# Memory attention and a gated feed-forward block on one core: block products for the first two batches too

## The chip, the cores and the metric

One NeuronCore of a Trainium2 chip runs the whole kernel in one launch. TensorE multiplies matrices into eight PSUM banks, ScalarE and VectorE evaluate functions and move PSUM to SBUF, GpSimd works on SBUF alone and also issues the casting loads, SyncE issues most stores. The metric is the device time of one execution in microseconds; the median over 3 runs of the kernel before is 238.54 (238.09 to 239.02).

## The reference

Inputs: q, k, v of shape 8 x 8 x 576 x 64 (batch, head, token, head dimension), phi of 8 x 8 x 576 x 32, and weights of 512 x 1536 (gate, value) and 1536 x 512 (output).

```
a    = softmax(phi, over the 32 memory slots)
k_m  = a^T k ;  v_m = a^T v                  # 32 x 64 per batch and head
attn = softmax(q k_m^T / 8)                  # 576 x 32
x    = attn v_m, heads side by side          # 4608 x 512
out  = (silu(x w_gate) * (x w_val)) w_out    # 4608 x 512, float32
```

## The kernel before

**Stages.** Batches are handled one after the other, except that batches 0 and 1 are interleaved. For a batch the kernel (1) sums keys and values over tokens with the softmax weights of phi (`kv_items`, matmuls at L235, scaled by `kv_norm`, transposed by `kv_T`), (2) computes scores (L400) and their exponentials E, (3) instead of forming x multiplies the value memory into the weights, U = v_m W (`u_round`, L471), (4) normalises E to A (`z_inv_v` and `norm`: L434, L441, L443, L451, all VectorE), (5) forms gate and value as A U in 24 slots of 128 rows x 288 tokens (`gv_slots`, L514), ScalarE's silu (L531) and VectorE's product (L537) giving the hidden tile h, transposed, in three chunks of 512 rows, and (6) multiplies h by the output weights.

**Two forms of the output step.** In batches 0 and 1 (`FAST = 2`) the 512 first tokens of a batch are four units of 12 matmuls of 512 columns (`out_units`, L633), one bank and one copy to SBUF (L333, L331) each. In batches 2 to 7 `products` (L713) uses the Strassen-Winograd scheme on 2 x 2 blocks: seven products instead of eight, 12 matmuls of 256 columns each. They need block sums of h (`chunk_done`: four operations per chunk, chunks 0 and 1 on GpSimd, chunk 2 on VectorE; L598, L560) and of the output weights (`weight_sums`, VectorE, once for all batches, tiles t_T). Three banks, s, a and c, collect the products; p1, q6 and p5 are copies to SBUF by ScalarE (L736), c11, c12 and c22 additions by VectorE (L741), c21 a copy. A product that starts in a bank waits until the copy or addition before it has read that bank. The last 64 tokens of two batches are one `out_rest` (L661).

**Order.** Each engine runs its instructions in the order in which the program lists them, and waits are semaphores set by the framework from the tiles. The order is written by hand: a list `backlog` holds the output units, `take(n)` places the next n of them, and `spread` merges gate/value slots, backlog and the next batch's preparation by position. `run_late` runs what `late` holds. PSUM banks are handed out in rotation by `bank` and `done`.

**Loads.** GpSimd issues all casting loads in program order; each also waits until the load eight before it has landed. Queries live in two slots (`Q_SLOT`): batches 2 and 3 share slot 0, so batch 3's load waits until batch 2's queries have been transposed, by a DMA issued from SyncE (`load_qT`, L121). Batches 0 and 1 are transposed on TensorE instead (`q_T`, L377, copied out at L388 and L390). Tiles of h, phi and keys/values have two buffers each; tiles of U and of block sums have one per chunk, tags U and S.

**The end.** `store` writes 128 rows in pieces that follow the output's layout; after `box["end"]` is set, pieces alternate between SyncE's and ScalarE's queues.

The order of the middle part before the change, which the edit rewrites:

```
load_qT(2); phi_exp(2)
run(take(16)); weight_sums(0); run(take(12))
run(kv_items(2)[:1] + take(6) + kv_items(2)[1:] + take(7))
weight_sums(1); run(take(11))
```

Of the kernel before, what the change touches and what calls it, by code (L numbers as in the profile page):

```python
# [14 lines left out]
def kernel(  # L15
# [66 lines left out]
        for t in tiles:  # L82
            free.append(held.pop(id(t))[0])

    Q_SLOT = (0, 1, 0, 0, 1, 0, 1, 0)

    def head_pairs(x):

# [370 lines left out]
    def u_round(b, parts, evac):  # L459


        banks = []
        for which, c, halves in parts:
            w0, w1, h0, h1 = which[0], which[-1] + 1, halves[0], halves[-1] + 1
            n = (h1 - h0) * HC
            p = [bank([128, CH], FP32, f"p_u{g}") for g in range(NG)]
            for w in which:
                o = (w - w0) * n
                for i in range(NP):
                    for g in range(NG):  # L470
                        nc.tensor.matmul(  # L471
                            p[g][32 * i:32 * i + 32, o:o + n],
                            lhsT=kTs[b][64 * g:64 * g + 64, 2, 32 * i:32 * i + 32],
                            rhs=w_part(w, c, i, g, halves),
                            start=True,
                            stop=True,
                            tile_position=(64 * g, 32 * i),
                        )
            for g in range(NG):
                if (b, c, g) not in Us:  # L480
                    Us[b, c, g] = upool.tile([128, 2, 2, HC], BF16, tag=f"U{c}{g}", name="t_U")
                if len(which) == 1:
                    dst = Us[b, c, g][:, h0:h1, w0]
                else:
                    dst = Us[b, c, g][:, h0]
                src = p[g][:, 0:(w1 - w0) * n].rearrange("p (a f) -> p a f", f=HC)
                banks.append((dst, src, p[g], rSs[b][:, g:g + 1] if b in scaled else None))
        for (t, p, home, r), e in zip(banks, evac):
            if e == "a":
                if r is None:  # L490
                    nc.scalar.copy(out=t, in_=p)  # L491
                else:
                    nc.scalar.activation(out=t, in_=p, func=AF.Copy, scale=r)
            elif r is None:
                nc.vector.tensor_copy(out=t, in_=p)  # L495
            else:
                nc.vector.tensor_scalar(out=t, in0=p, scalar1=r, scalar2=None, op0=ALU.mult)
            done(home)
# [48 lines left out]
        gv_gate(b, s)  # L547
        flush_mul(n)

    def u_buffers(b):  # L550

        for c in range(NCH):
            t = upool.tile([128, NG, 2, 2, HC], BF16, tag=f"S{c}", name="t_U")
            for g in range(NG):
                Us[b, c, g] = t[:, g]

    xs, Ss, late = {}, {}, []

# [22 lines left out]
    def chunk_done(b, c):  # L581

        if b % 2 == 0 and c == 0:
            xs[b // 2] = hpool.tile([128, NJF, 2, 64], BF16, tag="xs", name="t_x")

        def ends():
            nc.gpsimd.tensor_copy(
                out=xs[b // 2][:, 4 * c:4 * c + 4, b % 2], in_=hts[b, c][:, :, S - 64:S]
            )

        if b < FAST:
            ends()
            return
        eng = nc.vector if c + 1 == NCH else nc.gpsimd
        t = upool.tile([128, 4, 2, 256], BF16, tag=f"S{c}", name="t_S")
        Ss[b, c] = t
        A11, A12, A21, A22 = blocks(b, c)
        eng.tensor_tensor(out=t[:, 0], in0=A21, in1=A22, op=ALU.add)  # L598
        subtract(eng, t[:, 1], t[:, 0], A11)
        subtract(eng, t[:, 2], A11, A21)  # L600
        subtract(eng, t[:, 3], A12, t[:, 1])
        if c + 1 < NCH:
            ends()
        else:
            late.append(ends)

    def token_segments(b, t0, count):
        segs = []
# [8 lines left out]
    def store(t_o, b, t0, count, row=0, cols=slice(0, 512), queues=None):  # L617
# [3 lines left out]
        for n, (r0, m, bb, jj, pp) in enumerate(token_segments(b, t0, count)):  # L621
            eng = queues[n % len(queues)] if queues else nc.sync
            eng.dma_start(out=out_r[bb, jj, pp:pp + m, cols], in_=t_o[row + r0:row + r0 + m])

    def out_units(b, u, eng):

        mine = {}

        def unit(jf):
            def run():  # L630
                if jf == 0:
                    mine["p"] = bank([128, DM], FP32, "p_oo")
                nc.tensor.matmul(  # L633
                    mine["p"],
                    lhsT=hts[b, jf // 4][:, jf % 4, 128 * u:128 * (u + 1)],
                    rhs=WO[jf],
                    start=(jf == 0),
                    stop=(jf == NJF - 1),
                )
                if jf == NJF - 1:  # L640
                    t_o = work.tile([128, DM], FP32, tag="to", name="t_o")
                    copy(eng, t_o, mine["p"])
                    done(mine["p"])
                    store(t_o, b, 128 * u, 128)

            return run

        return [unit(jf) for jf in range(NJF)]

    def out_rest(pair, half):  # L650

# [31 lines left out]
    def products(b, by_hand):  # L683
# [56 lines left out]
        def add(out, home, other, free=False):  # L740
            nc.vector.tensor_tensor(out=out, in0=mine[home], in1=mine[other], op=ALU.add)  # L741
            if free:
                done(mine[home])

        def c11():
            t = tile_of("o1", (128, 2, DM), tag="to")
            add(t[:, :, lo], "a", "p1", True)

        def c22():
            t = tile_of("o2", (128, 2, DM), tag="to")  # L750
            add(t[:, :, hi], "s", "p5")

        def c12():
            t = mine["o1"]
            add(t[:, :, hi], "c", "q6", True)
            for u in range(2):
                store(t[:, u], b, 128 * u, 128)

        def c21():
            t = mine["o2"]  # L760
            copy("v" if box.get("end") else "a", t[:, :, lo], mine["s"])
            done(mine["s"])
            for u in range(2):
                store(t[:, u], b, 256 + 128 * u, 128)

        ops = dict(
            p1=keep("p1", "s"), q6=keep("q6", "s"), p5=keep("p5", "c"),
# [9 lines left out]
        if b + 1 == B:  # L777
            return first + six + five + seven + three + four, ops
        return first + five + six + three + seven + four, ops

    FAST = 2

    def out_list(b):
        res = []
        for u in range(4):
            res += out_units(b, u, "a" if u < 2 else "v")
        return res

    def q_items(b, evac):
        return [  # L790
# [86 lines left out]
    load_phi(2, nc.gpsimd)  # L877
    load_wo(2)
    load_v(2)
    load_phi(3, nc.gpsimd)  # L880
    load_q(2)
    load_q(3)
    u_buffers(1)


    warm(104)
# [51 lines left out]
        run([u_item(1, c)] + g0[s + 5:s + 8] + g1[s:s + 5])  # L938
    run(g1[-3:])
    flush_mul()  # L940
    backlog = out_list(0) + out_list(1) + out_rest(0, 0)

    def take(n):
        nonlocal backlog
# [1 line left out]
        part, backlog = backlog[:n], backlog[n:]  # L946
        return part

    KV = {b: 7 for b in range(3, B - 1)}

    def loads(b):

        if 4 < b + 1 < B:
            load_k(b + 1)
            load_v(b + 1)
        if b + 2 < B:
            load_q(b + 2)
            load_phi(b + 2, nc.gpsimd)

    def run_late():  # L960
        run(late)
# [4 lines left out]
    for b in range(2, B):  # L966
        last = b + 1 == B
        exp_tables()
        if b == 2:
            load_qT(2)  # L970
            phi_exp(2)
            run(take(16))
            weight_sums(0)
            run(take(12))
            run(kv_items(2)[:1] + take(6) + kv_items(2)[1:] + take(7))
            weight_sums(1)
            run(take(11))
        else:
            backlog += out_rest(b // 2 - 1, b % 2)
            run(take(6))  # L980
            loads(b)
        for g in range(NG):
            scores(b, g)
        if b > 2:
            ops["p1"]()
        u_values(b)
        if b == 2:
            load_k(3)
            load_v(3)
            load_q(4)  # L990
            load_phi(4, nc.gpsimd)
        else:
            run(take(6))
        z_inv_v(b, 0)
        norm(b, 0)
        if b > 2:
            ops["c11"]()
            run(take(6))
        if not last:
            phi_exp(b + 1)  # L1000
        z_inv_v(b, 1)
        norm(b, 1)
        if b > 2:
            run(take(6))
        run_late()
        nc.scalar.preload_act_table_set("silu_and_others")
        if b == 2:
            run(take(24))
            u_three(2)
            weight_sums(2)  # L1010
        run(take(12))
        g = gv_slots(b)
        beside = 0 if last else 7
        outs = [lambda: run(take(1)) for _ in range(len(backlog) - beside)]
        streams = [(g, 0, 24), (outs, 4 if b > 2 else 0, 24)]
        if last:
            streams += [([u_item(b, 2)], 5, 6)]
        if b == 2:
            streams += [
                ([lambda: load_qT(3)], 12, 12),  # L1020
                ([lambda: (load_k(4), load_v(4))], 12, 12),
                (kv_items(3, lambda: (u_item(2, 2, "aava")(), run(take(2)))), 12, 16),
                ([lambda: (run(take(2)), u_three(3), run(take(3)))], 17, 18),
            ]
        elif not last:
            load_qT(b + 1)
            phi_sum(b + 1)
            streams += [
                (kv_items(b + 1, lambda: (u_item(b, 2, "aava")(), run(take(2)))), KV[b], KV[b] + 4),
                ([lambda: (run(take(2)), u_three(b + 1), run(take(3)))], 19, 20),  # L1030
            ]
        spread(*streams)
# [4 lines left out]
    run(take(6))  # L1037
    ops["p1"]()
    run(out_rest(B // 2 - 1, 0))
    run(take(6))  # L1040
    ops["c11"]()
    box["end"] = True
    run(backlog)
    run(out_rest(B // 2 - 1, 1))
# [28 lines left out]
```

The softmax here doesn't subtract the row's maximum and nothing guards it: scores larger than these inputs give would overflow.

## Time and profile before

| what | value |
| --- | --- |
| median of 3 runs | 238.54 us |
| span of the profiled execution | 237.7 us |
| TensorE busy | 225.7 us, 95% |
| VectorE, ScalarE, GpSimd busy | 183.0, 169.5, 110.5 us |
| batches 0 and 1, first gate/value to last | 25.67 to 54.43 |
| their outputs and the preparation of batch 2 | 54.43 to 76.28 |
| gate and value slots of batch 2 | 76.28 to 93.75 |
| last matmul ends | 232.6 |
| last store is issued | 233.3 |

Profile lines give the start and length in us, the engine, the source line, the operation, the tile written and those read, shapes and how many instructions were merged; brackets give idle time before and what ended it. A table of stages gives, for each engine, busy time and the number of instructions. PEld is the loading of weights into TensorE, which overlaps its matmuls. A matmul's own length includes its way through the array, so the cost of one in a row is the distance between starts.

### The profile page before, as it was taken

The page shows a single profiled execution, that of the slowest core. Times are in us where ns is not written, and L with a number is a line of the kernel's source. Part 1 is how long each engine was busy: PE and PEld are TensorE (multiplying, and loading weights), DVE is VectorE, ACT ScalarE, POOL GpSimd, SP SyncE. Part 2 cuts the span into 40 slices and gives each one's busy share as a digit, 9 for nine tenths or more (in the row PEclk, how much of TensorE's full clock was granted, in tenths as well). Part 3 has the DMA queues.
Part 4 walks back from the last instruction along what each step waited for, and adds up shares of the span by engine and source line. Part 5 has one row for each costly group of instructions (what it writes and reads, how often), then busy time and mean ns, then how long its engine had stood idle before and what let it go on. Part 6 is the DMA issues. An engine that isn't in the chain of part 4 may idle for free.

```text
span 237.7 us, 7051 instructions
## 1 busy us (share of the span) xinstructions
PE 225.7 (95%) x2745; PEld 163.0 (69%) x2751; DVE 183.0 (77%) x410; ACT 169.5 (71%) x361; POOL 110.5 (47%) x149
## 2 busy tenths in 40 slices
PE   7988899999999999799999999999999999999991
PEld 2554467775544767587778777877788778878880
DVE  4247699995578888698789878988799879987621
ACT  2768889986067769687898779968897788677310
POOL 8523432000072297344992499167926492039400
PEclk9999999999999999999999999999999999999999
DMA  6999999998889999999169954999396621122206
GB/s 212 204 205 206 199 207 209 242 235 182 112 176 208 254 190 95 203 242 209 47 120 201 256 110 99 201 290 121 94 167 145 116 89 24 39 53 88 47 8 190
DMA packets 44592, 37.41 MB, mean 157 GB/s; under 512 B 17680, under 2 KB 39696, under 8 KB 44560
## 3 DMA queue, kind: packets, MB, share of 16 engines
q0 software_dynamic: 21424, 22.42, 56.2%
q1 hardware_dynamic: 22160, 13.38, 26.5%
q10 hardware_dynamic: 976, 1.18, 1.5%
q8 instruction: 21, 0.34, 0.6%
q14 instruction: 11, 0.09, 0.2%
HBM read 42.47 MB, written 9.44 MB: 218 GB/s over the span
## 4 chain that ended last, share of the span: by engine, by line
PE 65%; DMA 20%; DVE 7%; ACT 2%; issue 2%; POOL 2%; DVEq 0%; POOLq 0%
PE p_g L514 16%; PE p_v L514 15%; PE p_os L713 9%; PE p_oo L633 8%; DMA t_qT<-t_q 8%; DMA W<-in_moe_w_gate_dram 7%; PE p_u L471 4%; PE p_oc L713 4%; DMA t_kv<-in_k_dram 3%; PE p_oo L661 3%; PE p_oa L713 2%; DMA t_kT<-t_bkv 2%; ACT t_U L491 2%; PE p_kv L235 2%; DVE t_lz L443 1%
## 5 line engine op out<-in xcount | busy, mean ns | idle before, releaser
L537 DVE TENSOR_TENSOR t_h<-t_sg,p_v 128x288 bf16<-128x288 bf16 x192 | 83.7, 452 | 14.9 <-PE p_v L514 9.6
L514 PEld LDWEIGHTS <-t_U 128*128 128x128 bf16 x768 | 73.8, 98 | 22.2 <-issue 2.6
L531 ACT ACTIVATE t_sg<-p_g 128x288 bf16<-128x288 f32 x192 | 75.1, 420 | 18.8 <-PE p_g L514 11.8
L514 PE MATMUL p_g<-t_A,t_U 128*128 128x288 bf16 x384 | 77.1, 286 | 0.1
L514 PE MATMUL p_v<-t_A,t_U 128*128 128x288 bf16 x384 | 76.9, 286 | 0.0
L491 ACT CAST t_U<-p_u 128x512 bf16<-128x512 f32 x53 | 28.0, 607 | 8.4 <-PE p_u L471 8.4
L713 PEld LDWEIGHTS <-t_S 128*128 128x128 bf16 x288 | 28.2, 98 | 3.3
L598 POOL TENSOR_TENSOR t_S<-t_h 128x512 bf16<-128x512 bf16 x12 | 13.9, 1154 | 35.6 <-DVE t_h L537 35.6
L713 PEld LDWEIGHTS <-t_h 128*128 128x128 bf16 x216 | 20.4, 98 | 6.2 <-issue 3.2
L633 PE MATMUL p_oo<-WO,t_h 128*128 128x512 bf16 x90 | 21.6, 379 | 0.6 <-issue 0.5
L115 POOL DMA_DIRECT2D t_q<-in_q_dram x6 | 4.8, 798 | 32.2 <-DMA t_qT<-t_q 30.7
L713 PE MATMUL p_os<-t_T,t_S 128*128 128x256 bf16 x144 | 17.7, 273 | 0.0
L633 PEld LDWEIGHTS <-t_h 128*128 128x128 bf16 x96 | 9.0, 98 | 10.6 <-issue 1.1
L471 PE MATMUL p_u<-W,t_kT 64*32 64x512 bf16 (+1 forms) x416 | 16.0, 363 | 0.3 <-DMA W<-in_moe_w_gate_dram 0.2
L661 PE MATMUL p_oo<-WO,t_x 128*128 128x256 bf16 x96 | 14.5, 273 | 0.0
L560 POOL TENSOR_TENSOR t_S<-t_S,t_h 128x512 bf16<-128x512 bf16 x12 | 13.8, 1154 | 0.9
L560 POOL TENSOR_TENSOR t_S<-t_h,t_S 128x512 bf16<-128x512 bf16 x12 | 13.9, 1155 | 0.0
L560 POOL TENSOR_TENSOR t_S<-t_h 128x512 bf16<-128x512 bf16 x12 | 13.9, 1155 | 0.0
L836 PE MATMUL p_warm<-bones 128*128 128x512 bf16 (+2 forms) x43 | 12.1, 406 | 1.7 <-DVE bones L859 1.7
L495 DVE CAST t_U<-p_u 128x512 bf16<-128x512 f32 x19 | 12.4, 683 | 1.5 <-PE p_u L471 1.5
L451 DVE TENSOR_TENSOR t_A<-t_E,t_lz 128x576 bf16<-128x576 bf16 x16 | 12.1, 757 | 1.2 <-DVE t_lz L443 0.5
L411 ACT ACTIVATE t_E<-p_g 128x288 bf16<-128x288 f32 x12 | 5.0, 414 | 10.4 <-PE p_v L400 10.4
(93 smaller groups left out, 311.5 us busy)
## 6 DMA issues: line engine op xcount, KB each, us to landing
t_kv<-in_k_dram POOLq DMA_DIRECT2D x8, 576.0 KB, 8.1
t_kv<-in_v_dram POOLq DMA_DIRECT2D x8, 576.0 KB, 14.1
out_dram<-t_o SPq DMA_DIRECT2D x23, 192.0 KB, 2.9
t_phi<-in_phi_dram POOLq DMA_DIRECT2D x6, 576.0 KB, 16.3
t_q<-in_q_dram POOLq DMA_DIRECT2D x6, 576.0 KB, 10.8
out_dram<-t_o SPq DMA_DIRECT2D x36, 64.0 KB, 2.6
out_dram<-t_o SPq DMA_DIRECT2D x15, 128.0 KB, 3.8
WO<-in_moe_w_out_dram POOLq DMA_DIRECT2D x3, 512.0 KB, 18.8
```

The source lines that it names most:

```text
L451: nc.vector.tensor_tensor(out=a, in0=es.pop((b, g)), in1=lzs.pop((b, g)), op=ALU.mult)
L471: nc.tensor.matmul(p[g][32 * i:32 * i + 32, o:o + n], lhsT=kTs[b][64 * g:64 * g + 64, 2, 32 * i:32 * i + 32], rhs=w_part(w, c, i, g, halve ...
L491: nc.scalar.copy(out=t, in_=p)
L495: nc.vector.tensor_copy(out=t, in_=p)
L514: nc.tensor.matmul(p[:, 0:HALF], lhsT=Us[b, c, g][:, o // 2, which, 128 * (o % 2):128 * (o % 2 + 1)], rhs=atts[b, g][:, r], start=(g == 0) ...
L531: nc.scalar.activation(out=sg, in_=gate[:, 0:HALF], func=AF.Silu)
L537: nc.vector.tensor_tensor(out=dst, in0=sg, in1=val[:, 0:HALF], op=ALU.mult)
L560: eng.tensor_tensor(out=out, in0=x, in1=y, op=ALU.subtract)
L598: eng.tensor_tensor(out=t[:, 0], in0=A21, in1=A22, op=ALU.add)
L633: nc.tensor.matmul(mine["p"], lhsT=hts[b, jf // 4][:, jf % 4, 128 * u:128 * (u + 1)], rhs=WO[jf], start=(jf == 0), stop=(jf == NJF - 1),)
L661: nc.tensor.matmul(mine["p"], lhsT=xs[pair][:, jf].rearrange("p a t -> p (a t)"), rhs=WO[jf][:, cols], start=(jf == 0), stop=(jf == NJF - 1),)
L713: nc.tensor.matmul(mine[home][:, u], lhsT=lhs(c, m, u), rhs=rhs(c, m), start=fresh and u == 0, stop=(k == 5), skip_group_check=u == 1 or n ...
```

## The change

It gives batches 0 and 1 the seven products that later batches have, and makes room for what that needs.

1. `out_units`, `out_list` and `FAST` go. `chunk_done` makes block sums for batches 0 and 1: GpSimd for chunks 0 and 1, VectorE for chunk 2. The sums of batch 0's chunks 1 and 2 are put off (`late`) to the stage after 54.43, since their tiles take the buffers that batch 1's U still holds; batch 1's sums take batch 0's U buffers.
2. The loads of phi 3, queries 2 and 3, keys and values 3 are issued by GpSimd between its blocks of sums (`beside_sums`) instead of in one row. Queries of batch 2 come in two halves.
3. Batch 2's queries are transposed on TensorE (24 transposes, four copies to SBUF), not by DMA; `Q_SLOT` now alternates, so batches 2 and 3 no longer share a slot.
4. In later stages queries, phi, keys and values are all loaded two batches ahead, and the preparation of batch 3 stands in batch 2's slots where later batches have theirs.
5. At the very end each quarter block (256 of 512 columns) is stored as soon as it is done, not each half.

```diff
-    Q_SLOT = (0, 1, 0, 0, 1, 0, 1, 0)
+    Q_SLOT = (0, 1, 0, 1, 0, 1, 0, 1)
...
-        if b < FAST:
-            ends()
-            return
-        eng = nc.vector if c + 1 == NCH else nc.gpsimd
-        t = upool.tile([128, 4, 2, 256], BF16, tag=f"S{c}", name="t_S")
+        t = upool.tile([128, 4, 2, 256], BF16, tag=f"U{c}" if b == 1 else f"S{c}", name="t_S")
...
+        end = c + 1 == NCH
+        if b == 0 and c > 0:
+            late.append(lambda: sums(nc.vector if end else nc.gpsimd))
+        else:
+            sums(nc.vector if end else nc.gpsimd)
...
+        if (b, c) in beside_sums:
+            beside_sums[b, c]()
+
+    beside_sums = {
+        (0, 0): lambda: (load_phi(3, nc.gpsimd), load_q_group(2, 0)),
+        (1, 0): lambda: (load_q_group(2, 1), load_q(3)),
+        (1, 1): lambda: (load_k(3), load_v(3)),
+    }
...
         def c11():
             t = tile_of("o1", (128, 2, DM), tag="to")
             add(t[:, :, lo], "a", "p1", True)
+            if box.get("end"):
+                both("o1", 0, lo)
...
-    load_phi(3, nc.gpsimd)
-    load_q(2)
-    load_q(3)
...
-    backlog = out_list(0) + out_list(1) + out_rest(0, 0)
+    backlog = []
...
     def loads(b):
-        if 4 < b + 1 < B:
-            load_k(b + 1)
-            load_v(b + 1)
         if b + 2 < B:
             load_q(b + 2)
             load_phi(b + 2, nc.gpsimd)
+            load_k(b + 2)
+            load_v(b + 2)
...
         if b == 2:
-            load_qT(2)
             phi_exp(2)
-            run(take(16))
+            (one, ops1), (zero, ops0) = products(1, ("c11",)), products(0, ("p1",))
+            kv, q2 = kv_items(2), q_items(2, "aava")
+            run(one[:6])
             weight_sums(0)
-            run(take(12))
-            run(kv_items(2)[:1] + take(6) + kv_items(2)[1:] + take(7))
             weight_sums(1)
-            run(take(11))
+            run(one[6:12] + zero[:6] + kv[:1] + q2[:2])
+            weight_sums(2)
+            ops1["c11"]()
+            run(one[12:18] + kv[1:] + q2[2:])
+            ops0["p1"]()
+            late.pop()()
+            mark = att.tile([1, 1], BF16, tag="mark", bufs=1, name="t_mark")
+            nc.gpsimd.tensor_copy(out=mark, in_=kTs[2][0:1, 0, 0:1])
+            run_late()
+            run(one[18:24])
+            backlog = zero[6:] + one[36:] + out_rest(0, 0)
...
+        else:
+            run(one[24:36])
         u_values(b)
         if b == 2:
-            load_k(3)
...
+            u_three(2)
+            load_qT(3)
+        run(take(6))
         z_inv_v(b, 0)
         norm(b, 0)
...
-        run(take(12))
+        run(take(18 if b == 2 else 12))
...
     run(out_rest(B // 2 - 1, 0))
+    box["end"] = True
     run(take(6))
     ops["c11"]()
-    box["end"] = True
```

The one-element copy `mark` reads batch 2's key transpose; it keeps GpSimd's delayed block of sums from starting before that tile is written. In `products` the six units k = 0 to 5 of a product are two units per chunk; the order is p1, a, five, six, three, seven, four (the last batch: p1, a, six, five, seven, three, four). Product four adds to the bank s, after c22 has read it.

More of the change, by code (lines that the diff above doesn't have):

```diff
@@ L480, in u_round @@
                 if (b, c, g) not in Us:
-                    Us[b, c, g] = upool.tile([128, 2, 2, HC], BF16, tag=f"U{c}{g}", name="t_U")
+                    u_buffer(b, c, f"U{c}")
                 if len(which) == 1:
@@ L548, in gv_slot, with u_buffer @@
         flush_mul(n)
[L550 to L555, printed above, removed]
+    def u_buffer(b, c, tag):
+        t = upool.tile([128, NG, 2, 2, HC], BF16, tag=tag, name="t_U")
+        for g in range(NG):
+            Us[b, c, g] = t[:, g]
     xs, Ss, late = {}, {}, []
@@ L589, in ends, with sums @@
             )
-        if b < FAST:
-            ends()
-            return
-        eng = nc.vector if c + 1 == NCH else nc.gpsimd
-        t = upool.tile([128, 4, 2, 256], BF16, tag=f"S{c}", name="t_S")
+        t = upool.tile([128, 4, 2, 256], BF16, tag=f"U{c}" if b == 1 else f"S{c}", name="t_S")
         Ss[b, c] = t
         A11, A12, A21, A22 = blocks(b, c)
[L598 to L602, printed above, removed]
-            ends()
-        else:
-            late.append(ends)
+        def sums(eng):
+            eng.tensor_tensor(out=t[:, 0], in0=A21, in1=A22, op=ALU.add)
+            subtract(eng, t[:, 1], t[:, 0], A11)
+            subtract(eng, t[:, 2], A11, A21)
+            subtract(eng, t[:, 3], A12, t[:, 1])
+        end = c + 1 == NCH
[3 more added lines that the diff above has]
+            sums(nc.vector if end else nc.gpsimd)
+        if end and b > 1:
+            late.append(ends)
+        else:
+            ends()
+        if (b, c) in beside_sums:
[5 more added lines that the diff above has]
+    }
     def token_segments(b, t0, count):
@@ L623, in store @@
             eng.dma_start(out=out_r[bb, jj, pp:pp + m, cols], in_=t_o[row + r0:row + r0 + m])
[L625 to L648, printed above, removed]
     def out_rest(pair, half):
@@ L743, in add, with both @@
                 done(mine[home])
+        def both(name, t0, cols):
+            for u in range(2):
+                store(mine[name][:, u, cols], b, t0 + 128 * u, 128, cols=cols)
         def c11():
@@ L751, in c22 @@
             add(t[:, :, hi], "s", "p5")
+            if box.get("end"):
+                both("o2", 256, hi)
         def c12():
@@ L755, in c12 @@
             add(t[:, :, hi], "c", "q6", True)
-            for u in range(2):
-                store(t[:, u], b, 128 * u, 128)
+            both("o1", 0, hi if box.get("end") else slice(0, DM))
         def c21():
@@ L762, in c21 @@
             done(mine["s"])
-            for u in range(2):
-                store(t[:, u], b, 256 + 128 * u, 128)
+            both("o2", 256, lo if box.get("end") else slice(0, DM))
         ops = dict(
@@ L779, in products @@
         return first + five + six + three + seven + four, ops
[L781 to L787, printed above, removed]
     def q_items(b, evac):
@@ L879 @@
     load_v(2)
-    load_phi(3, nc.gpsimd)
-    load_q(2)
-    load_q(3)
-    u_buffers(1)
+    for c in range(NCH):
+        u_buffer(1, c, f"S{c}")
     warm(104)
@@ L947, in take @@
         return part
-    KV = {b: 7 for b in range(3, B - 1)}
+    KV = 7
     def loads(b):
-        if 4 < b + 1 < B:
-            load_k(b + 1)
-            load_v(b + 1)
         if b + 2 < B:
@@ L980 @@
             run(take(6))
-            loads(b)
+        loads(b)
         for g in range(NG):
@@ L985 @@
             ops["p1"]()
+        else:
+            run(one[24:36])
         u_values(b)
         if b == 2:
-            load_k(3)
[L989 to L993, printed above, removed]
+            u_three(2)
+            load_qT(3)
+        run(take(6))
         z_inv_v(b, 0)
@@ L997 @@
             ops["c11"]()
-            run(take(6))
+        run(take(6))
         if not last:
@@ L1002 @@
         norm(b, 1)
-        if b > 2:
-            run(take(6))
+        run(take(6))
         run_late()
         nc.scalar.preload_act_table_set("silu_and_others")
[L1007 to L1010, printed above, removed]
-        run(take(12))
+        run(take(18 if b == 2 else 12))
         g = gv_slots(b)
@@ L1014 @@
         outs = [lambda: run(take(1)) for _ in range(len(backlog) - beside)]
-        streams = [(g, 0, 24), (outs, 4 if b > 2 else 0, 24)]
+        streams = [(g, 0, 24), (outs, 4, 24)]
         if last:
             streams += [([u_item(b, 2)], 5, 6)]
-        if b == 2:
+        if not last:
+            if b > 2:
+                load_qT(b + 1)
+                phi_sum(b + 1)
             streams += [
[L1020 to L1029, printed above, removed]
+                (kv_items(b + 1, lambda: (u_item(b, 2, "aava")(), run(take(2)))), KV, KV + 4),
                 ([lambda: (run(take(2)), u_three(b + 1), run(take(3)))], 19, 20),
```

## The prediction

> **What bounds the kernel now.** I read the page first (busy shares, slices, chain), then TensorE's waits, then busy time stage by stage, then the timelines of TensorE, VectorE and GpSimd around the stages that the edit touches.
>
> ```profile
> PE 225.7 (95%) x2745; PEld 163.0 (69%) x2751; DVE 183.0 (77%) x410; ACT 169.5 (71%) x361; POOL 110.5 (47%) x149
> PEclk9999999999999999999999999999999999999999
> ...
> PE 65%; DMA 20%; DVE 7%; ACT 2%; issue 2%; POOL 2%; DVEq 0%; POOLq 0%
> ```
>
> TensorE is busy 95% of the span at an unthrottled clock and is two thirds of the chain. So the time is TensorE's work plus TensorE's few waits plus a head and a tail. TensorE's list of waits has only one large entry after the start:
>
> ```profile
> PE p_g L400 <- DMA t_qT<-t_q: 1.7, 1, 1.7
> ```
>
> By stage (start:end, length, then busy time of each engine):
>
> ```profile
> 54.43:76.28 21.85, 21.43 (x219) 9.99 (x220) 14.46 (x33) 11.49 (x19) 5.88 (x11) 1.00 0.92 160
> 76.28:93.75 17.47, 17.25 (x240) 12.72 (x241) 14.17 (x33) 13.06 (x32) 11.23 (x12) 1.00 1.28 191
> 93.75:104.04 10.29, 8.62 (x99) 7.31 (x97) 8.16 (x16) 7.58 (x13) 2.10 (x4) 1.00 1.28 181
> 104.04:120.70 16.66, 16.66 (x236) 12.71 (x234) 13.82 (x32) 13.24 (x33) 12.87 (x17) 1.00 0.64 158
> ```
>
> 54.43 is where TensorE finishes the gate and value products of batches 0 and 1; up to 76.28 it computes their outputs and prepares batch 2. VectorE has 14.46 us of work there in 21.85, so 7 us free. In the third row TensorE is idle 1.67 us; in the fourth, a later batch, not at all. The idle piece is this one:
>
> ```profile
> 93.75 1.47 PE L713 MATMUL p_os<-WO,t_h 128*128 128x256 bf16 x12
> 96.89 0.28 PE L400 MATMUL p_g<-t_qT,t_kT 64*32 64x288 bf16 x1 [1.67 <-DMA t_qT<-t_q]
> ```
>
> The first line is also a price: one of the seven products, 12 matmuls of 256 columns. Neighbouring products start 1.31 us apart (97.48, 98.80, 100.11), so a product costs 1.31. The 512-column matmuls of L633 advance 23 in 4.96 us, 0.2156 each.
>
> **What the Trainium skill says.** "SBUF — State Buffer", section Who interferes with whom: a VectorE instruction with two SBUF inputs and a GpSimd instruction that reads SBUF share one read interface, held for a whole instruction, and the loser blocks. The trace of before agrees in one short meeting:
>
> ```profile
> 173.01 0.51 POOL L587 COPY t_x<-t_h 128x256 bf16<-128x256 bf16 x1
> ...
> 173.19 0.61 DVE L560 TENSOR_TENSOR t_S<-t_h 128x512 bf16<-128x512 bf16 x1
> 173.73 0.41 DVE L560 TENSOR_TENSOR t_S<-t_h,t_S 128x512 bf16<-128x512 bf16 x1
> ```
>
> The VectorE subtraction took 0.61 beside the copy and its twin 0.41 alone. The multiplications of L537, with one input in PSUM, take 454 ns beside GpSimd's sums (82 to 86) and the same without (106 to 108). "TensorE: Matmul & The Clock Gate", section on the 16 sub-arrays: VectorE's, ScalarE's and GpSimd's queues are strict FIFO. I rest on this below: work behind a waiting instruction waits too. The same SBUF page, The DMA setup-cost knee: a transfer pays about 2 us whatever its size; here the quickest store of 222 to 238 landed in 1.9.
>
> **The change part by part.**
>
> *Eight 512-wide matmul groups become seven products.* Removed: two batches x 4 units x 12 matmuls = 96 x 0.2156 = 20.70. Added: 2 x 7 x 1.31 = 18.34. TensorE: -2.36. It is on the path, as TensorE has no slack here.
>
> *Queries of batch 2 on TensorE.* 24 transposes; 12 advance TensorE by 0.52 (19.11 to 19.63, L377). +1.04, on the path. In return the transposing DMA of batch 2 goes and batches 2 and 3 no longer share a slot. In before GpSimd stood 26.27 us, to 67.06, waiting for that transpose before it could issue batch 3's load, whose transpose then landed at 96.89. Now batch 3's load goes out about 50 and its transpose about 70; with transposes landing in a median of 7.7 us that is long before the 95 us at which TensorE wants it. -1.67. About 0.2 of idle TensorE in the second stage should go too, as its stream gets the shape of later batches.
>
> *GpSimd's sums of batches 0 and 1.* A block of four takes 4 x 1.15 = 4.6:
>
> ```profile
> 81.69 1.16 POOL L598 TENSOR_TENSOR t_S<-t_h 128x512 bf16<-128x512 bf16 x1 [8.75 <-DVE t_h L537]
> 82.92 1.15 POOL L560 TENSOR_TENSOR t_S<-t_S,t_h 128x512 bf16<-128x512 bf16 x1
> 84.03 1.16 POOL L560 TENSOR_TENSOR t_S<-t_h 128x512 bf16<-128x512 bf16 x1
> 85.15 1.16 POOL L560 TENSOR_TENSOR t_S<-t_h,t_S 128x512 bf16<-128x512 bf16 x1
> ```
>
> Three blocks run between 37 and 55, where GpSimd had 42 to 54 empty. Loads queue behind them: the two halves of batch 2's queries go out at about 43 and 49 instead of 40. The DMA engines were full to 57 (the load issued at 40.0 took 20.0 us), so later issue costs no bandwidth; I expect landings near 58 and 60, against uses at 59.6 and 62.1. Cost zero, hidden by TensorE's output work; up to 1.0 if a half is late.
>
> *VectorE between 54.4 and 77.* This is where I expect the change to pay back. VectorE gets two blocks of sums (4 operations started in 1.5 each, as weight sums run from 55.20 to 56.7) and six additions of L741's kind (0.69) in place of four 0.69 copies. Walk it along. TensorE: three products to 58.36, key and value sums 1.25 (60.48 to 61.73 in before), 12 transposes, so product five begins at 60.13 and its third chunk at 61.0. It needs the third weight sum. VectorE: from 55.20 sums, weight sums 0 and 1 (4.5) to 59.7, reciprocal and norms 1.2 (61.62 to 62.82), first operation of weight sum 2 0.42: 61.3, plus some tenths for GpSimd copies. TensorE waits 0.5.
> Then TensorE: five done 61.9, transposes 0.7, six 1.31, scores 0.26, three and seven 2.62, to 66.8; values of U 0.35; then three rounds of U at once. The latter need banks freed by ScalarE (copies 0.47 apart) and by VectorE's addition c12 of batch 1. The ScalarE part alone stops TensorE 0.9 (0.67 on the bank, 0.2 on the next). Ahead of c12 stand the four sums of batch 0's last chunk, from 63.9; GpSimd starts its own delayed block at 63.7, released by the key transpose just before. Alone, VectorE's sums end at 65.4 and c12 is in time. In full alternation, 4.6 + 1.5 from 63.7, they end at 69.8 and TensorE waits 2.9. The trace does not show four against four; runs of independent operations on either side can keep the port, so I take the middle: they end at 68.6 and TensorE waits 1.9.
> Last, batch 0. After its product "a", VectorE must do c11 0.69, two softmax chains of 2.60 (68.16 to 70.76), c12 and c22 0.69 each: 7.3. TensorE has four products, 5.24, before product four, whose bank c22 frees. It waits 2.0; nothing else is queued on TensorE that could go first.
> New waits: 0.5 + 1.9 + 2.0 = 4.4 (3.4 to 5.4).
>
> *Tail.* TensorE ends at 232.6, the last stores start at 233.1 and land about 2.8 later, with the DMA engines full from 231.5 to 235.5. Half of 1 MB now leaves 1.3 us and more earlier, so the last stores should land in about 2.1: -0.7 (-0.4 to -0.9). The added stores on ScalarE's queue stand before one copy (q6), which has about 0.5 us to spare: zero.
>
> *Loads of keys and values two batches ahead, kv items of batch 2 at 7, slot parity:* zero; later stages have the same loads and no idle TensorE.
>
> Sum: -2.36 + 1.04 - 1.67 - 0.2 - 0.7 + 4.4 = +0.5. 238.54 + 0.5 = 239.0, no measurable change. With the sums not colliding 238.0, in full alternation 240.0.
>
> **The rivals.** *Faster, 236.0.* The gains hold (-4.9 + 1.0) and new waits come to only 1.4, because VectorE overlaps more than starts in the trace let me count. For it: VectorE had 7 us free in the stage and every gain but the tail is read off TensorE directly. Against: the wait of product four needs only FIFO order and measured durations, and alone is 2.0. *Slower, 240.8.* Full alternation (5.4 of waits) and a half of the queries 0.8 late: 238.5 - 3.9 + 5.4 + 0.8. For it: the port rule and the 0.61 above, and the 20 us load. Against: independent operations can slip in together.
>
> **How the numbers follow.** Forecast (237.4 to 239.7) 0.42, faster rival 0.27, slower rival 0.31. The known ends are 238.0 and 240.0; reaching into both rivals until two in ten are left gives 236.2 to 240.9.
>
> **What would show it.** TensorE's wait of 1.7 on t_qT gone, 96 matmuls of 512 columns gone and 168 of 256 more; a stage after 54.4 with VectorE busy over 90% and TensorE idle some 4 us; a wait of product four's bank on VectorE's addition near 78; VectorE's sums at 64 to 69 far above 0.41 each beside GpSimd's. Wrong if these sums stay at 0.4, if TensorE waits on t_q near 60, or if TensorE shows under 2 us idle before the slots of batch 2.

## The result and the profile after

The changed kernel takes **241.38 us** (median of 4 runs, 240.93 to 242.39) against 238.42 (238.09 to 239.02) before: a ratio of 1.0127, interval 1.0089 to 1.0166. It is slower by 3.0 us. The forecast was 239.0 with a range of 236.2 to 240.9; the time lies above the range, beside the slower rival (240.8).

The head of the page of the changed kernel, the counterpart of the first lines shown of before (busy time, granted clock, chain):

```profile
PE 227.0 (94%) x2847; PEld 171.9 (71%) x2847; DVE 191.6 (80%) x421; ACT 172.9 (72%) x368; POOL 130.2 (54%) x167
PEclk9999999999999799999999999999999999999999
...
PE 79%; DMA 10%; DVE 5%; POOL 2%; issue 1%; SPq 1%; DVEq 0%; POOLq 0%
```

TensorE is busy for 227.0 us, before it was 225.7, although seven products stand in place of eight; 24 transposes were added, and a part of it is matmuls at a lower clock, which has a dent in the fourteenth slice (78 to 84 us). Its waits, the largest first (L699 is a product, L727 an addition into the output tile, L559 a block sum; p_warm and p_mT belong to the start):

```profile
PE p_os L699 <- DVE t_o L727: 2.4, 1, 2.4
PE p_warm L820 <- DVE bones L843: 1.7, 1, 1.7
PE p_u L471 <- DVE t_o L727: 1.7, 1, 1.7
PE p_mT L319 <- DMA t_kv<-in_v_dram: 1.0, 1, 1.0
PE p_oc L699 <- DVE t_T L559: 0.9, 1, 0.9
```

Before, the only large wait after the start was one of 1.7 on batch 3's transposed queries. It is gone, and three waits on VectorE, 0.88 + 1.68 + 2.40 = 4.96 us, stand in its place. They show on TensorE's timeline in brackets, and so does what follows the last:

```profile
60.03 1.04 PE L699 MATMUL p_oc<-t_T,t_S 128*128 128x256 bf16 x8
61.95 0.60 PE L699 MATMUL p_oc<-t_T,t_S 128*128 128x256 bf16 x4 [0.88 <-DVE t_T L559]
...
67.57 0.82 PE L471 MATMUL p_u<-W,t_kT 64*32 64x512 bf16 x17
70.06 0.62 PE L471 MATMUL p_u<-W,t_kT 64*32 64x512 bf16 x15 [1.68 <-DVE t_o L727]
...
75.87 1.47 PE L699 MATMUL p_os<-t_T,t_S 128*128 128x256 bf16 x12
79.74 2.04 PE L699 MATMUL p_os<-t_T,t_h 128*128 128x256 bf16 x12 [2.40 <-DVE t_o L727]
81.57 1.17 PE L514 MATMUL p_g<-t_A,t_U 128*128 128x288 bf16 x4
```

Product five stops after its second chunk, the rounds of U stop in the middle, product four stops before it begins. Product four then advances 1.83 (79.74 to 81.57), where the others advance 1.31.

### The profile page after: what moved, and what is told of

Its sections match the earlier page's. It is cut to its first block, busy times and chain, and to the rows that moved or that the text cites. A ratio compares the mean times of both kernels' runs of the same rounds, so it can differ in the third digit from the quotient of the medians.

```text
span 240.6 us, 7296 instructions
## 1 busy us (share of the span) xinstructions
PE 227.0 (94%) x2847; PEld 171.9 (71%) x2847; DVE 191.6 (80%) x421; ACT 172.9 (72%) x368; POOL 130.2 (54%) x167
## 4 chain that ended last, share of the span: by engine, by line
PE 79%; DMA 10%; DVE 5%; POOL 2%; issue 1%; SPq 1%; DVEq 0%; POOLq 0%
PE p_g L514 20%; PE p_v L514 19%; PE p_os L699 16%; DMA t_kv<-in_v_dram 7%; PE p_oc L699 7%; PE p_u L471 5%; PE p_oo L647 5%; PE p_oa L699 3%; DMA out_dram<-t_o 3%; PE p_kv L235 2%; DVE t_h L537 1%; DVE t_T L559 1%; POOL t_q L108 1%; PE p_g L400 1%; POOL t_kv L98 1%
## 5 line engine op out<-in xcount | busy, mean ns | idle before, releaser
L514 PE MATMUL p_g<-t_A,t_U 128*128 128x288 bf16 x384 | 77.9, 289 | 0.0
L595 POOL TENSOR_TENSOR t_S<-t_h 128x512 bf16<-128x512 bf16 x16 | 18.4, 1152 | 45.7 <-DVE t_h L537 45.7
L699 PEld LDWEIGHTS <-t_S 128*128 128x128 bf16 x384 | 37.3, 98 | 5.6 <-issue 1.3
L699 PEld LDWEIGHTS <-t_h 128*128 128x128 bf16 x288 | 27.4, 98 | 10.6 <-issue 6.5
L699 PE MATMUL p_os<-t_T,t_S 128*128 128x256 bf16 x192 | 23.6, 273 | 0.0
L559 POOL TENSOR_TENSOR t_S<-t_S,t_h 128x512 bf16<-128x512 bf16 x16 | 18.5, 1158 | 1.3
L699 PE MATMUL p_os<-t_T,t_h 128*128 128x256 bf16 x96 | 16.5, 281 | 2.4 <-DVE t_o L727 2.4
L559 POOL TENSOR_TENSOR t_S<-t_h,t_S 128x512 bf16<-128x512 bf16 x16 | 18.6, 1165 | 0.0
L559 POOL TENSOR_TENSOR t_S<-t_h 128x512 bf16<-128x512 bf16 x16 | 18.6, 1164 | 0.0
L699 PE MATMUL p_oc<-t_T,t_S 128*128 128x256 bf16 x96 | 12.0, 273 | 0.9 <-DVE t_T L559 0.9
L699 PE MATMUL p_oa<-WO,t_h 128*128 128x256 bf16 x96 | 11.9, 273 | 0.0
```

The source lines that it names most:

```text
L514: nc.tensor.matmul(p[:, 0:HALF], lhsT=Us[b, c, g][:, o // 2, which, 128 * (o % 2):128 * (o % 2 + 1)], rhs=atts[b, g][:, r], start=(g == 0) ...
L559: eng.tensor_tensor(out=out, in0=x, in1=y, op=ALU.subtract)
L699: nc.tensor.matmul(mine[home][:, u], lhsT=lhs(c, m, u), rhs=rhs(c, m), start=fresh and u == 0, stop=(k == 5), skip_group_check=u == 1 or n ...
```

## The experiments

All runs are of one core; "after" is the changed kernel. Ratios are to the kernel before on the same chip.

**1. Product four last (e1_four), 2. the two sums apart (e2_apart), 3. both (e3_both).** The order of the backlog, and the tile that GpSimd's delayed sums wait for:

```diff
-            backlog = zero[6:] + one[36:] + out_rest(0, 0)
+            backlog = zero[6:36] + one[36:] + zero[36:] + out_rest(0, 0)     # e1, e3
-            nc.gpsimd.tensor_copy(out=mark, in_=kTs[2][0:1, 0, 0:1])
+            nc.gpsimd.tensor_copy(out=mark, in_=Ss[0, 2][0:1, 3, 0, 0:1])    # e2, e3
```

In e1 batch 1's product four goes ahead of batch 0's, so that c22 has 1.31 us more. In e2 GpSimd starts only when VectorE's four sums are done.

> Product four of batch 1, whose bank has long been read, takes the place of product four of batch 0 ahead of the slots; four of batch 0 moves among the slots. Waits theory: TensorE's wait of 2.40 us on VectorE's addition goes, and with it the half clock that followed (0.50 from 81 to 83); 237 to 238, some 3 to 4 below the changed kernel. Rival (the loss is in the products themselves or in the loads two batches ahead): the place of one product doesn't matter, 241.

> The mark that releases GpSimd's delayed block reads the last result of VectorE's sums instead of the key transpose, so the two blocks run one after the other. Port theory: VectorE's four sums fall from 1.35 to about 0.4 us each, TensorE's wait of 1.68 in the rounds of U goes to 0.9 at most, and all behind it is earlier by 1 to 2: 239.5 to 240.5. Rival (the sums were slow for another reason, such as their data): they stay above 1 us each, 241 or more.

> Both edits. Waits theory: the gains add in part, 236 to 237, faster than before. Rival: no better than the better of the two alone.

Measured: e1 238.57 (238.03 to 240.2), ratio 1.0002 (0.9981 to 1.0023); e2 239.44 (239.23 to 240.07), 1.0034 (1.0017 to 1.0052); e3 237.63 (237.29 to 239.4), 0.9957 (0.9935 to 0.9978). Against after that is -2.8, -1.9 and -3.8 us. The causes of the last two waits are shown by removing them. What e2 undoes is seen on VectorE's timeline of after, then on GpSimd's, same stretch:

```profile
64.17 1.35 DVE L595 TENSOR_TENSOR t_S<-t_h 128x512 bf16<-128x512 bf16 x1
65.56 1.26 DVE L559 TENSOR_TENSOR t_S<-t_S,t_h 128x512 bf16<-128x512 bf16 x1
66.75 1.37 DVE L559 TENSOR_TENSOR t_S<-t_h 128x512 bf16<-128x512 bf16 x1
68.04 1.37 DVE L559 TENSOR_TENSOR t_S<-t_h,t_S 128x512 bf16<-128x512 bf16 x1
69.33 0.68 DVE L727 TENSOR_TENSOR t_o<-p_oc,t_q 128x512 f32<-128x512 f32 x1
```

```profile
64.10 1.14 POOL L595 TENSOR_TENSOR t_S<-t_h 128x512 bf16<-128x512 bf16 x1
65.32 1.22 POOL L559 TENSOR_TENSOR t_S<-t_S,t_h 128x512 bf16<-128x512 bf16 x1
66.51 1.33 POOL L559 TENSOR_TENSOR t_S<-t_h 128x512 bf16<-128x512 bf16 x1
67.80 1.32 POOL L559 TENSOR_TENSOR t_S<-t_h,t_S 128x512 bf16<-128x512 bf16 x1
```

One VectorE sum gets through for every GpSimd sum. The addition behind them, c12 at 69.33, ends at 70.01, and TensorE resumes at 70.06. On VectorE in e2 the same four take:

```profile
64.23 0.42 DVE L595 TENSOR_TENSOR t_S<-t_h 128x512 bf16<-128x512 bf16 x1
64.68 0.42 DVE L559 TENSOR_TENSOR t_S<-t_S,t_h 128x512 bf16<-128x512 bf16 x1
65.02 0.42 DVE L559 TENSOR_TENSOR t_S<-t_h 128x512 bf16<-128x512 bf16 x1
65.35 0.42 DVE L559 TENSOR_TENSOR t_S<-t_h,t_S 128x512 bf16<-128x512 bf16 x1
66.48 0.69 DVE L727 TENSOR_TENSOR t_o<-p_oc,t_q 128x512 f32<-128x512 f32 x1 [0.71 <-ACT t_E L411]
```

c12 now starts 2.85 earlier, about when product three, which it adds, ends (66.37; the bracket names an exponential of ScalarE's that ended at 66.43). What is left on TensorE there is a wait of 0.32 for ScalarE's copy of U. TensorE's waits in e3, those of the start and a last one of 0.2 left out:

```profile
PE p_oc L699 <- DVE t_T L559: 0.9, 1, 0.9
PE p_g L400 <- DVE t_qT L390: 0.5, 2, 0.3
PE p_u L471 <- DVE t_kT L333: 0.5, 1, 0.5
PE p_u L471 <- ACT t_U L491: 0.3, 1, 0.3
```

Both large waits are gone. In size the expectations were a little off: e1 and e3 came out 0.6 above theirs, e2 just below. The gains, 2.8 and 1.9, are near the waits removed: 2.40 in e1; in e2 1.68 less 0.32, and 0.47 of product four's wait, which fell to 1.93 as c22 no longer waits for an output buffer.

**4. Keeping TensorE awake (e4_warm).** 11 matmuls of 512 columns on constants fill the wait before product four; nothing reads their result.

```diff
-        run(take(18 if b == 2 else 12))
+        run(take(12))
+        if b == 2:
+            warm(44)
+            run(take(6))
```

> 11 matmuls of 512 columns on constants stand between products seven and four, some 2.4 us of work in the wait; nothing else is changed, the results are the same. Clock theory: the wait on VectorE stays about as long in time, but TensorE keeps its clock at 1.00 and product four and the first slots are not stretched: 1 to 2 below the changed kernel, 239.5 to 240.5. Rival (the half clock costs nothing since VectorE or ScalarE would hold the slots anyway): 241.4.

Measured: 240.95 (240.61 to 241.52), ratio 1.0093 (1.0065 to 1.0121), 0.4 below after. That is less than expected, and with an interval of 1.0089 to 1.0166 for after it is not clear of noise. What was expected of the clock is seen in the traces. First after, then e4 (columns: stretch, length, busy time of TensorE, weight load, VectorE, ScalarE and GpSimd, granted clock, DMA share, GB/s):

```profile
79.50:81.00 1.50, 1.26 (x10) 1.05 (x10) 0.19 (x1) 0.00 (x0) 0.00 (x0) 0.83 1.20 197
81.00:83.00 2.00, 2.00 (x10) 1.30 (x9) 0.00 (x0) 1.12 (x3) 0.00 (x0) 0.50 1.20 196
83.00:85.00 2.00, 2.00 (x14) 1.47 (x13) 1.21 (x3) 1.12 (x4) 0.00 (x0) 0.77 1.20 198
```

```profile
81.00:83.00 2.00, 2.00 (x19) 1.63 (x17) 0.67 (x2) 1.60 (x5) 0.00 (x0) 1.00 1.20 197
```

The clock falls to half after the wait in the one and stays at 1.00 in the other, with 19 matmuls in 2 us in place of 10. The miss is in how often: the drop is not in every execution of after, whose mean clocks were 0.993, 1.000, 0.990 and 0.998. In e1 five of 22 executions took 240.0 to 240.2 with a mean clock of 0.993, and the others 238.0 to 238.9 with 0.997 to 1.000. So a drop costs some 1.6 when it comes (medians 240.08 and 238.47), about what 3.4 us at half the clock lose; on after's median it is perhaps 0.4. In e1, where the wait of 2.40 is gone, the dent stands behind the wait of 1.68 that ends at 70.29:

```profile
71.00:73.00 2.00, 2.00 (x12) 1.46 (x11) 1.10 (x2) 1.31 (x3) 1.38 (x2) 0.54 0.95 91
```

Why a wait drops the clock in one execution and not in the next can be read from where the clock changes. It was at half from 80.50 to 83.91 in after, 71.14 to 74.55 in e1 and 62.43 to 65.84 in e6 (below): 3.41 each. Within each trace all changes lie a multiple of 3.413 apart, and the first falls anywhere from 4.4 to 7.0 after the start. Cut into such steps, after holds its whole wait of 2.40 in one step, and the next is at half; in a_notail (below), whose clock changes at 6.79 and 238.90 alone, an edge at 78.47 cuts the wait of 2.22 into 1.08 and 1.14, and the clock stays. First after, then a_notail:

```profile
77.09:80.50 3.41, 1.01 (x10) 0.76 (x8) 2.18 (x4) 0.00 (x0) 0.00 (x0) 1.00 1.17 232
80.50:83.91 3.41, 3.41 (x17) 2.28 (x15) 0.45 (x1) 1.49 (x4) 0.00 (x0) 0.50 1.20 197
```

```profile
75.06:78.47 3.41, 2.33 (x22) 1.94 (x20) 3.31 (x6) 1.89 (x3) 0.00 (x0) 1.00 1.10 337
78.47:81.88 3.41, 2.27 (x20) 1.95 (x20) 0.89 (x2) 0.76 (x2) 0.00 (x0) 1.00 1.21 199
```

In all traces of this study, once the clock was full, every step with 1.90 or more of idle TensorE was followed by half rate, one (e1) of the seven with 1.66 to 1.70, and none with less. Why e1's 1.68 was enough is open. This is read from traces; no run moved a wait against the steps on purpose.

**5. Before once more (b_again).** Nothing is changed.

> The kernel before, unchanged, for a second trace: its profiled execution (239.53) was 1.1 above its median. If the wait on the transposed queries of batch 3 varies, it is well under 1.67 us here, and the prediction's gain from taking it away was oversized; if it is a fixed cost, it is 1.6 to 1.7 again and the difference lies elsewhere.

Measured: 238.25 (one execution), span 236.4. TensorE's largest waits, and its last product before the scores of batch 3 with the first of these scores:

```profile
PE p_warm L836 <- DVE bones L859: 1.7, 1, 1.7
PE p_g L400 <- DVE t_qT L390: 0.5, 2, 0.3
PE p_oo L633 <- issue: 0.5, 3, 0.2
```

```profile
93.90 1.47 PE L713 MATMUL p_os<-WO,t_h 128*128 128x256 bf16 x12
95.30 0.29 PE L400 MATMUL p_g<-t_qT,t_kT 64*32 64x288 bf16 x1
```

**There is no wait on batch 3's transposed queries.** Their transpose landed 14.7 us after its issue at 77.94; in the first trace it was 19.1 after 77.79, and in b_tail below, where this part of the kernel is unchanged, 15.0 after 78.06. Landing near 93, it is there 2 us before the use at 95.3. The first trace was of an execution of 239.53, one above its median, and TensorE ended 1.7 later in it than here (232.58, 230.87), as much as that wait. Why the transpose landed late there is open.

**6. The slots alone (b_slots).** Before, with batches 2 and 3 in different query slots, but batch 2 still transposed by DMA.

```diff
-    Q_SLOT = (0, 1, 0, 0, 1, 0, 1, 0)
+    Q_SLOT = (0, 1, 0, 1, 0, 1, 0, 1)
```

> The kernel before with alternating query slots alone, so that batch 3's load no longer waits for batch 2's transpose. By the prediction's term: 1.67 below before, 236.7, no wait on t_qT in the trace. Rival (the typical execution waits less, or the earlier load takes the time elsewhere): 0 to 0.8 below, 237.5 to 238.3.

Measured: 245.57 (244.82 to 246.12), ratio 1.0288 (1.0260 to 1.0316). Both expectations missed. TensorE's waits in b_slots, and then SyncE's issue of batch 2's transpose there and in b_again:

```profile
PE p_g L400 <- DMA t_qT<-t_q: 5.1, 1, 5.1
```

```profile
59.99 7.99 SPq L121 DMA_TRANSPOSE t_qT<-t_q  x1
```

```profile
59.79 3.07 SPq L121 DMA_TRANSPOSE t_qT<-t_q  x1
```

Batch 3's load now goes out at 42.7 in place of 66.9, and the loads of keys and values at 56.1 and 56.8 in place of 69.8 and 70.5. They fill the DMA engines while batch 2's transpose runs (their share, which this view can put above 1, is 1.24 to 1.63 from 60 to 66, in b_again 0.69 to 0.87), and TensorE waits 5.06 for it. Then the clock was at half until 77.15; TensorE worked at it from 72.38, which costs half of that time, some 2.4 by estimate. The old slot order had kept these loads away. Whether it is bandwidth or a queue that the transpose loses was not tried.

**7. The stores alone (b_tail).** Before, with only the quarter-block stores at the very end.

```diff
+            if box.get("end"):
+                both("o1", 0, lo)
...
-            for u in range(2):
-                store(t[:, u], b, 128 * u, 128)
+            both("o1", 0, hi if box.get("end") else slice(0, DM))
...
+    box["end"] = True
     run(take(6))
     ops["c11"]()
-    box["end"] = True
```

> The kernel before with the stores at the very end by quarter block alone. By the prediction's term: 0.7 below before (0.4 to 0.9), 237.4 to 237.9. Rival (the end is a fixed latency after the last store): no change, 238.3.

Measured: **236.89** (236.68 to 237.3), ratio 0.9930 (0.9906 to 0.9954): -1.5, twice the expected gain, and the fastest kernel of the study. SyncE's wait for its last stores, in b_again and then in b_tail (total, times, longest):

```profile
SPq L1068 <- DMA out_dram<-t_o: 3.1, 2, 2.8
```

```profile
SPq L1074 <- DMA out_dram<-t_o: 1.7, 2, 0.9
```

The stores now begin earlier and no longer crowd: from 230 to 232 and from 232 to 234 the DMA engines' busy share was 0.93 and 0.90 in b_again, 0.72 and 0.55 in b_tail. Earlier stores and smaller ones were not tried apart.

**8. Transposes first (e5_best).** e3 with all four groups of batch 2's transposes ahead of product five, copied out by ScalarE.

```diff
-            kv, q2 = kv_items(2), q_items(2, "aava")
+            kv, q2 = kv_items(2), q_items(2, "aaaa")
-            run(one[6:12] + zero[:6] + kv[:1] + q2[:2])
+            run(one[6:12] + zero[:6] + kv[:1] + q2)
...
-            run(one[12:18] + kv[1:] + q2[2:])
+            run(one[12:18] + kv[1:])
```

> The version with both edits (block sums one after the other, product four of batch 1 first), and now all four transposes of batch 2's queries ahead of product five, copied by ScalarE alone, to fill TensorE's wait of 0.88 on the third weight sum and take the copy of the queries off VectorE. Waits theory: 0.5 to 0.8 below the version with both, 236.8 to 237.1. Rival (the second half of the queries is not there yet, or ScalarE is late): equal or slower, 237.6 or more.

**9. The weight sum first (e6_sums).** e5, with the third weight sum ahead of the norms on VectorE, and product six ahead of the key transposes.

```diff
             weight_sums(1)
+            weight_sums(2)
             run(one[6:12] + zero[:6] + kv[:1] + q2)
-            weight_sums(2)
             ops1["c11"]()
-            run(one[12:18] + kv[1:])
+            run(one[12:18])
             ops0["p1"]()
+            run(one[18:24] + kv[1:])
             late.pop()()
...
-            run(one[18:24])
```

> The repaired version with the third weight sum placed ahead of the norms on VectorE, all four groups of query transposes ahead of product five, and product six ahead of the key transposes. If the wait of 0.9 before product five is only a matter of VectorE's order, it goes and the time is 236.8. Rival: VectorE is full in this stretch, the wait moves on to the key transposes or the scores, and the time stays at 237.6.

Measured: e5 237.71 (237.44 to 242.09), ratio 0.9967 (0.9955 to 0.9980), no better than e3; e6 240.99 (239.95 to 241.39), 1.0107 (1.0079 to 1.0135), 3.4 above e3. Neither gain came. The wait of 0.9 on the third weight sum is gone from both traces, but the last query transposes wait instead for VectorE's norms of keys and values (L271), 1.0 in e5 and 2.5 in e6. So these two orders only move the wait. VectorE was busy 1.93 to 2.00 of each 2 us from 56 to 68 in after; that it is simply full is the likely reason, and not shown apart. The wait in e5, then in e6:

```profile
PE p_q L377 <- DVE t_bkv L271: 1.0, 1, 1.0
```

```profile
PE p_q L377 <- DVE t_bkv L271: 2.5, 1, 2.5
```

In e6 the clock fell as well, from 62.43 to 65.84: the next product took 2.64 where one takes 1.47.

**10, 11. After and e3 with the old tail (a_notail, e3_notail).** The reverse of the edit of b_tail.

> The changed kernel with the old tail: halves stored whole, two queues only from the last units on, as before the change. If the tail's stores and the middle part add up, this is 1.5 above the changed kernel, 242.9, and the middle part alone costs 4.4 over before. If the tail hides part of the middle part's loss, it is under 242.

> The repaired version (product four last, the delayed sums of GpSimd after those of VectorE) with the old tail. Theory: the repaired middle part is worth about +0.7 over before, as its three remaining waits (0.9, 0.5, 0.3) and the 1.0 of transposes eat the 2.4 of the seven products, so 239.1, and all of the repaired version's gain is the tail. Rival: the middle part gains by itself, then 238.4 or less.

Measured: a_notail 242.54 (242.31 to 243.09), ratio 1.0182 (1.0165 to 1.0199); e3_notail 239.24 (238.91 to 240.68), 1.0044 (1.0025 to 1.0062). The first lies between its two cases, the second is as expected. So the middle part alone costs 4.1 in after, and 0.8 even when it is repaired. All that e3 gains over before is its tail.

## Why the prediction was wrong, step by step

a_notail gives the account without tail, and its profiled execution kept the clock at 1.00 after a last wait of 2.22. From the end of batch 1's slots to the scores of batch 3, I added TensorE's distances from start to start, idle time apart, in a_notail and in b_again. The first row compares, in b_again, units 20.12, batch 2's first product 1.40 and idle 0.48 with the same work in a_notail, 20.28.

| part | predicted | measured |
| --- | --- | --- |
| seven products for eight, with the 0.2 of idle in the slots | -2.56 | -1.72 (22.00 to 20.28) |
| 24 transposes | +1.04 | +1.03 |
| wait for batch 3's queries | -1.67 | 0 |
| new waits | +4.4 (3.4 to 5.4) | +4.79 (0.88, 1.69, 2.22) |
| everything else | 0 | -0.04 |
| sum up to batch 3's scores | +1.2 | +4.06 (scores at 99.28 against 95.30: 3.98) |
| tail | -0.7 | -1.2 (after against a_notail) to -1.6 (e3 against e3_notail); b_tail -1.5 |

- **The step that failed** is "-1.67" for batch 3's queries: "Now batch 3's load goes out about 50 and its transpose about 70", which "is long before the 95 us at which TensorE wants it". That came true (49.3, and the transpose at 72.8 landed 14.5 later), and the wait is gone, but b_again and b_tail, two further traces of this part of before, do not have it. A gain was subtracted from a median that, as far as these traces tell, did not contain the loss. This alone is more than half of the error of 2.4.
- **The products** were over-sized by 0.8. Some 0.6 of it lies in their price: 15 products (14, and batch 2's first) took 20.28, where 15 times 1.31 is 19.65. 1.31 is the price of a product between others of its kind; one ahead of scores or rounds of U takes 1.41 (63.06 to 64.47 and 66.16 to 67.57 in after), and ahead of a wait its whole length of 1.47 counts. The other 0.2 is the idle time that was to go, which probably was none. The gaps "issue" of 0.16 in before stand in rows of L633, where the trace records 96 weight loads and only 90 matmuls; behind one such gap it has five matmuls where the program places six. The prediction's 1.25 for key and value sums (60.48 to 61.73) contains this gap: in after they took 1.03 (58.48 to 59.51).
- **The new waits** were right in place, cause and order, 4.79 to 4.96 for 4.4. Product five: 0.88 for 0.5, as some of VectorE's first sums took 0.50 and 0.61 beside GpSimd. The c12 wait: "in full alternation ... they end at 69.8", "so I take the middle: they end at 68.6"; they ended at 69.41. Neither engine kept the port for more than one of its sums; the middle had no ground in the trace, the end did. TensorE itself came 0.8 later too (at 68.4, where 69.8 + 0.7 - 2.9 meant 67.6), so it waited 1.68 and not 2.9, and that 1.68 stands so near the forecast 1.9 is luck. Product four: 2.0 was counted; after has 2.40 because c22 also waited 0.38 for an output buffer still being stored.
- **The tail** was mis-sized by half: -0.7 for -1.2 to -1.6, with the range -0.4 to -0.9 too narrow. The reckoning took 2.8 for the landing of the last stores (the last two of the first trace took 3.1); in b_again those on ScalarE's queue, used only at the end, landed in 3.0 to 3.9, and in b_tail in 2.0 to 2.2. In b_tail TensorE ends at 231.25 and the span 4.1 later, in b_again at 230.87 and 5.5 later.
- **Not in the sum:** the half-rate clock after a wait, some 1.6 where it comes (e1), and on after's median perhaps 0.4 (e4, not clear of noise).
- Of the rivals, the slower one named full alternation rightly; its late query half did not happen: the halves landed at 58.2 and 59.8, and after's trace has no wait on t_q near 60.
- Loads, kv items and slot parity at "zero" held: the remainder is -0.04. b_slots shows that the parity without the transposes on TensorE costs 7.1; the transposes without the parity were not tried.

The rule of the Trainium skill that the prediction used, "SBUF — State Buffer", Who interferes with whom, that VectorE's two-input operations contend with GpSimd's reads, agrees with after and e2 (1.26 to 1.37 beside GpSimd's sums, 0.42 apart). The Trainium skill, "TensorE: Matmul & The Clock Gate", Part 1, says that the clock falls to half after at least one idle window of about 3.4 us, and that these windows run freely. The length of 3.41 and the varying first edge agree, but a window need not be idle throughout: 2.40 was enough in after, 1.90 in e6 and 1.68 in e1. Here the measurement decides.

## What to carry to other kernels

Before subtracting a wait that a change removes, see whether the profiled execution is as long as the median, and look for the wait in a second trace: a wait that ends on a transfer may belong to one execution. Moving multiplications off TensorE by block sums puts work on VectorE; where VectorE's stretch is nearly full (23.86 of 25 us from 54.5 to 79.5 in after), products whose bank or operand VectorE must serve become waits. Reordering took two of these away (e1, e2) and only moved the third (e5, e6). VectorE's and GpSimd's two-input sums should not run side by side when something on the path stands behind one of them: a later start of GpSimd's gained 1.9 us at no cost.

## What was not expected of the hardware

- TensorE's granted clock changes on a grid of 3.41 us whose place differs from execution to execution. A step with 1.90 or more of idle time was always followed by one at half rate, one with 1.66 to 1.70 once in seven. So a wait of some 2 us can cost 1.6 us more, in some executions only (five of 22 in e1).
- VectorE's and GpSimd's sums alternate one for one when both have a row of them: 0.42 becomes 1.26 to 1.37 on VectorE, and GpSimd's 1.15 becomes at most 1.33.
- In b_slots a transposing DMA beside loads took 7.99 us to issue, in b_again 3.07, and TensorE waited 5.1 us for it.
- Stores of a quarter block in place of a half, at the very end, were worth 1.5 us (b_tail): those on ScalarE's queue landed in medians of 2.0 to 2.2 in place of 3.0 to 3.9.
